# Retention attention and a SwiGLU block on one core: the second tile's attention ticks placed at other steps

## The chip, the cores and the metric

The kernel runs on one core of one Trainium2 chip. The metric is the device time of one execution in microseconds. Engines are named as in the profile: PE (matmuls), DVE (VectorE), ACT (ScalarE), POOL (GpSimd) and SP (the queue that issues most loads and stores).

## The reference

Eight batches of eight heads, 576 positions of 64 values each, go through a retention layer: scores `q k^T / 8`, multiplied with a decay that falls with the distance, times `v`. The result, seen as 4608 tokens of 512 values, is the input x of a SwiGLU block with 1536 hidden values.

```python
ret = scale * (q @ k.transpose(0, 1, 3, 2)) * Dmat      # Dmat[h, i, j] = gamma[h] ** (i - j) for i >= j, else 0
x = (ret @ v).transpose(0, 2, 1, 3).reshape(4608, 512)
g = x @ w_gate
out = (g * sigmoid(g) * (x @ w_val)) @ w_out
```

All data are float32.

## The kernel before

**Attention.** Two heads of a batch make a pair; there are 32 pairs, four to a batch. Each pair is cut into 9 chunks of 64 positions; a running state carries the earlier chunks. The work is pipelined in ticks: `tick(t)` (L675) prepares pair t, does the scores and the new states of pair t-1, and the values of pair t-2. PE's part is emitted at once where the tick stands, in this order: values of pair t-2 from its own scores (L531), new states of t-1 from its k and v (L542), values from earlier states of t-2 (L554, L558), scores of t-1 from qT and kT (L566, L572). It is some 2.2 us of 64x64 matmuls.

The rest of a tick is a list of pieces for the other engines, handed out little by little. For the ticks in question they are, in this order:

- P0: ACT copies the even states (L583), DVE masks the scores (L579, L588), ACT copies the finished values to x (L646, L621);
- P1, in three parts: DVE pairs states up (L593); DVE runs the odd states (three of L598); DVE the even states (L603) and ACT scales k (L506) and, below pair 20, q (L486);
- P2: DVE transposes q into qT (L489);
- P3: DVE transposes k into kT (L489), and SP gets the loads of pair t+2. The one kT buffer serves all pairs.

A tick that begins flushes what is left of the one before.

**SwiGLU.** The tokens are worked through in five tiles; tile 0 is handled apart. In the others the matmuls of a tile are done as a fast bilinear scheme: 26 products per quarter of the hidden values in the up direction (`up_step`, L976, 8 matmuls of 128x256, 1.73 us), three quarters, and then 26 products down (`down_step`, L1030, 12 matmuls, 2.59 us). The tables `UP` and `DOWN` give for each product its PSUM bank, the sums and differences of operands ahead of it, and what is read out of the bank behind it. Reads that take a bank's value are DVE additions (L929) or ACT copies (L926), the hidden values are products of DVE (L1016, L1019) behind an ACT activation (L1013). Sums of operands are L795 and L963 on POOL or DVE. SP also fetches stored operands through a ring of eight places, one at each down step.

**Where the two meet.** Tile 1 (the second tile, `n == 1`) is the one that this change is about: its weight sums are computed while it runs. The first 26 up steps are done without ticks. Here the other 52 are called u0 to u51 (u0 to u25 the second quarter, u26 to u51 the third), and the down steps d0 to d25. Among them stand ticks 12 to 21. Tick 12 has no PE work.

The order in which instructions are emitted is the order on each engine. Around an up step it is: sums for x and weights; the 8 matmuls; if a tick came just ahead, its P0 (`after_tick`); the reads; one part of the next piece (`part_on`), unless the table's line of this step or of the next has five or more reads. The line of the eighteenth step of a quarter (counted from 0) has seven, so u17, u18, u43 and u44 hand out nothing beyond a P0. Around a down step it is: sums of hidden values; 12 matmuls; the fetch; P0 if a tick came just ahead; the reads; and then up to three whole pieces (`go_on(3)`), which is all that a tick has left.

So a tick ahead of u17 leaves P0 at u17, the parts of P1 at u19, u20 and u21, P2 at u22, and P3 at the end of u23.

Of the kernel before, what the change touches and what calls it, by code (L numbers as in the profile page):

```python
# [154 lines left out]
def kernel(  # L155
# [101 lines left out]
    def needed(n):  # L257

        last = (min(starts[n] + TW, NT) - 1) // S
        return last * HP + HP - 1 + 3  # L260
# [547 lines left out]
    for line in OUT_SUMS:  # L808
        i, s = line.split("|")
# [220 lines left out]
    def down_step(n, i):  # L1030
        label, opens, slot, hops, ops = down[i]
        for op in hops:
            add(nc.gpsimd if i % 3 == 1 and op[0] != "nad" else nc.vector, op, hid_view)
        w = operand().rearrange("p (q x) -> p q x", q=NQ)
        lhs = hid_view(slot)
        b = bank(label, i == 0)
        for qd in range(NQ):
            for m in range(2):
                nc.tensor.matmul(b[:, m * TB : (m + 1) * TB], lhs[:, qd, ts(m, P)], w[:, qd],  # L1039
                                 start=(opens and qd == 0 and m == 0), stop=(qd == NQ - 1), skip_group_check=True)  # L1040
        fetch()

        def result(o, src, negative, vector):
            if negative:
                nc.scalar.mul(out=src, in_=src, mul=-1.0)
            d, t = divmod(o, 4)
            rows = starts[n] + t * TB
            nc.sync.dma_start(out=out[rows : rows + TB, d * TB : (d + 1) * TB].rearrange("(m p) d -> p m d", p=P),
                              in_=src.rearrange("p (m d) -> p m d", m=2))

        if n + 1 == NTILE and i + 1 == N:
            _, o, a = ops.pop()
            d, t = divmod(int(o), 4)
            at, rows = part[int(a)], starts[n] + t * TB
            assert ops == [["add", a, "b", a]]
            for m, queue in enumerate((nc.sync, nc.scalar)):
                nc.vector.tensor_tensor(out=at[:, ts(m, TB)], in0=b[:, ts(m, TB)], in1=at[:, ts(m, TB)], op=ALU.add)
                queue.dma_start(out=out[rows + m * P : rows + (m + 1) * P, d * TB : (d + 1) * TB], in_=at[:, ts(m, TB)])
            return
        after_tick()  # L1060
        reads(ops, b, False, result)
        at = 2 * (i - (N - 1 - X_FIRST // 2))
        if 0 <= at < X_FIRST and n + 1 < NTILE:
            x_sums(n + 1, at, at + 2, True)
        go_on(3)


    def merge(*lists):
        merged = [((i + d) / len(l), j, f) for j, (d, l) in enumerate(lists) for i, f in enumerate(l)]
        for _, _, f in sorted(merged, key=lambda e: e[:2]):  # L1070
            f()
# [73 lines left out]
    done = FIRST  # L1145

    def spread_tick(t):
        tick(t, FIRST, NP, True, lambda: next_load(t))
        fresh.append(t)

    ticks = lambda a, b: [lambda t=t: spread_tick(t) for t in range(a, b)]
    for n in range(1, NTILE):
        upto = needed(n + 1) if n + 1 < NTILE else done
        cut = (done + upto + (n == 1) * 2) // 2
        ups = [lambda qd=qd, i=i: up_step(n, qd, i) for qd in range(NQ) for i in range(N)]
        if n == 1:

            for i in range(N):
                ups.pop(0)()
                if i in (6, 14):  # L1160
                    wait = nc.sync.nop()
                    tc.add_manual_dep(wait.ins, stepped[-1].ins.name,
                                      mybir.DependencyInfo(mybir.DependencyClass.Sync, mybir.DependencyReason.DATA), reason="loads in turn")
                    load(FIRST + i // 14)
        downs = [lambda i=i: down_step(n, i) for i in range(N)]
        merge((0.0, ticks(done, cut)), (0.5, ups))
        if n == 1:

            for i, f in reversed(list(zip((2, 7, 13, 19), ticks(cut, upto), strict=True))):
                downs.insert(i, f)  # L1170
            merge((0.5, downs))
        else:
            merge((0.0, ticks(cut, upto)), (0.5, downs))
        done = upto

# [29 lines left out]
```

## Time and profile before

| | us |
|---|---|
| median of 3 runs | 1048.08 |
| lowest and highest | 1047.18, 1050.52 |
| the profiled execution, its own time | 1047.18 |
| its span, first to last instruction | 1045.5 |
| PE busy | 1027.6 (98%) |
| DVE, POOL, ACT busy | 653.9, 401.9, 297.2 |
| granted TensorE clock, mean | 0.998 |

Start times of PE's work in the profiled execution, in us from the span's start: u0 at 222.54, tick 13 at 238.17, tick 14 at 253.38, u24 at 269.03, tick 15 at 272.65, u26 at 275.63, tick 16 at 291.37, tick 17 at 307.64, d0 at 327.22, tick 18 at 332.49, tick 19 at 347.90, tick 20 at 366.40, tick 21 at 384.40, the end of the tile near 405.6.

How to read the lines that follow: a timeline line has the start and the length in us, the engine, the line of the kernel, the operation, what it writes and reads, its shape and how many instructions were merged; in brackets the idle time of the engine ahead of it and what ended that. A line of stretches has, after the stretch and its length, busy time and count of PE, PE's weight loads, DVE, ACT and POOL, then the granted clock, the share of the DMA engines and GB/s.

### The profile page before, as it was taken

To read this page: it belongs to the slowest core of one execution; us is meant where nothing else is said; L and a number is where in the kernel's file an instruction comes from. 1 tells how busy PE (TensorE), PEld (TensorE's weight loads), DVE (VectorE), ACT (ScalarE), POOL (GpSimd) and SP (SyncE) were. 2 spreads that over 40 slices of the span, in tenths; PEclk is the share of its full clock that TensorE was granted. 3 is DMA by queue.
4 is the path that set the end of the run, shared out by engine and by line. 5 is a ranking of instruction groups with operands and counts; after the bars stand their busy time and mean duration, and the time that the engine had idled before them with its cause. 6 is when DMAs were issued, how large, how long until landed. Compare 5 with 4: busy or idle time off the path is not lost.

```text
span 1045.5 us, 21496 instructions
## 1 busy us (share of the span) xinstructions
PE 1027.6 (98%) x8448; PEld 843.9 (81%) x8448; DVE 653.9 (63%) x1063; ACT 297.2 (28%) x646; POOL 401.9 (38%) x347
## 2 busy tenths in 40 slices
PE   7999999999999999999999999999999999999998
PEld 6444555888888888888888888888888888888887
DVE  4678878777769757555357786535476644344644
ACT  3466423243533222232322102223120022231110
POOL 2002367767476035612223048312250483222505
PEclk9999999999999999999999999999999999999999
DMA  9999867776678887665676777545554565555653
GB/s 248 242 283 258 198 197 267 207 212 182 186 204 227 239 249 200 193 178 149 176 220 159 214 182 220 154 136 155 154 174 140 153 200 152 152 153 161 181 161 101
DMA packets 310380, 199.10 MB, mean 190 GB/s; under 512 B 220168, under 2 KB 254984, under 8 KB 310280
## 3 DMA queue, kind: packets, MB, share of 16 engines
q1 hardware_dynamic: 279000, 161.51, 57.2%
q10 hardware_dynamic: 31280, 36.22, 10.4%
q8 instruction: 67, 1.10, 0.5%
q14 instruction: 33, 0.27, 0.1%
HBM read 157.56 MB, written 40.11 MB: 189 GB/s over the span
## 4 chain that ended last, share of the span: by engine, by line
PE 76%; DVE 4%; DMA 1%; ACT 0%; issue 0%; POOL 0%; ACTq 0%; DVEq 0%
PE bankC L992 12%; PE bankE L992 12%; PE bankA L992 11%; PE bankB L992 11%; PE bankA L1039 6%; PE bankB L1039 6%; PE bankC L1039 6%; PE bankE L1039 6%; DVE rest L929 1%; PE outer L531 1%; PE inner L572 1%; DVE state L598 1%; PE outer L558 1%; PE inner L542 1%; DVE arena L1016 1%
## 5 line engine op out<-in xcount | busy, mean ns | idle before, releaser
L929 POOL TENSOR_TENSOR rest<-rest 128x512 f32<-128x512 f32 x65 | 92.1, 1421 | 296.7 <-DVE rest L929 277.9
L1013 ACT ACTIVATE io<-rest 128x256 f32<-128x256 f32 x180 | 74.9, 416 | 305.3 <-DVE rest L929 259.1
L992 PE MATMUL bankA<-rest,arena 128*128 128x256 f32 x544 | 128.9, 380 | 1.8 <-DVE rest L929 1.0
L992 PE MATMUL bankC<-rest,arena 128*128 128x256 f32 x544 | 129.2, 380 | 1.4 <-DVE rest L929 1.4
L795 POOL TENSOR_TENSOR arena<-arena 128x512 f32<-128x512 f32 (+1 forms) x72 | 112.5, 1574 | 38.3 <-DMA up<-arena 22.4
L992 PE MATMUL bankE<-rest,arena 128*128 128x256 f32 x512 | 121.4, 380 | 1.0 <-DVE rest L929 1.0
L992 PE MATMUL bankB<-rest,arena 128*128 128x256 f32 x512 | 121.2, 379 | 0.0
L992 PEld LDWEIGHTS bankA<-rest,arena 128*128 128x128 f32 x544 | 103.0, 190 | 16.9 <-issue 1.9
L1020 POOL TENSOR_TENSOR arena<-rest,io 128x256 f32<-128x256 f32 x72 | 52.1, 729 | 167.3 <-ACT io L1013 167.3
L992 PEld LDWEIGHTS bankC<-rest,arena 128*128 128x128 f32 x544 | 102.8, 190 | 16.3 <-issue 1.8
L992 PEld LDWEIGHTS bankE<-rest,arena 128*128 128x128 f32 x512 | 97.0, 190 | 14.7 <-DVE rest L929 1.4
L992 PEld LDWEIGHTS bankB<-rest,arena 128*128 128x128 f32 x512 | 97.0, 190 | 13.4 <-issue 0.2
L795 POOL TENSOR_TENSOR rest<-rest 128x256 f32<-128x256 f32 (+1 forms) x66 | 67.8, 1048 | 100.9 <-DVE rest L419 61.2
L929 DVE TENSOR_TENSOR rest<-bankB,rest 128x512 f32<-128x512 f32 x72 | 48.8, 686 | 65.6 <-PE bankB L992 49.7
L929 DVE TENSOR_TENSOR rest<-bankC,rest 128x512 f32<-128x512 f32 x72 | 48.9, 687 | 64.6 <-PE bankC L992 45.9
L929 DVE TENSOR_TENSOR rest<-bankA,rest 128x512 f32<-128x512 f32 x72 | 48.8, 685 | 61.1 <-PE bankA L992 43.5
L929 DVE TENSOR_TENSOR rest<-bankE,rest 128x512 f32<-128x512 f32 x71 | 48.2, 687 | 60.5 <-PE bankE L992 46.1
L1016 DVE SCALAR_TENSOR_TENSOR arena<-rest,io 128x256 f32<-128x256 f32 x84 | 57.8, 689 | 11.1 <-ACT io L1013 10.9
L1039 PE MATMUL bankC<-arena 128*128 128x256 f32 x252 | 58.4, 381 | 0.3 <-issue 0.3
L1039 PE MATMUL bankB<-arena 128*128 128x256 f32 x252 | 58.3, 381 | 0.0
L1039 PE MATMUL bankA<-arena 128*128 128x256 f32 x252 | 58.0, 380 | 0.2 <-DVE arena L795 0.2
L1039 PE MATMUL bankE<-arena 128*128 128x256 f32 x252 | 57.9, 379 | 0.0
(189 smaller groups left out, 1632.4 us busy)
## 6 DMA issues: line engine op xcount, KB each, us to landing
arena<-up SPq DMA_DIRECT2D x234, 256.0 KB, 2.7
arena<-dn SPq DMA_DIRECT2D x104, 384.0 KB, 3.9
up<-arena ACTq DMA_DIRECT2D x78, 256.0 KB, 4.1
dn<-rest SPq DMA_DIRECT2D x78, 128.0 KB, 1.9
out_dram<-rest SPq DMA_DIRECT2D x31, 256.0 KB, 3.7
qk<-in_q_dram SPq DMA_DIRECT2D x108, 72.0 KB, 2.4
qk<-in_k_dram SPq DMA_DIRECT2D x108, 72.0 KB, 3.1
rest<-in_moe_w_out_dram ACTq DMA_DIRECT2D x6, 1024.0 KB, 5.4
```

Source lines behind the costliest of these rows:

```text
L531: m = nc.tensor.matmul(value(i, hl, c), s["v"][rows, at], ret[rows, c % 2 if whole(i) else hl, c // 2], start=start, stop=start, skip_grou ...
L542: nc.tensor.matmul(z[half[hl], r, c], s["kn"][chunk(i, hl, 2 * c + r, i < HP)], s["v"][rows, at], start=True, stop=True, skip_group_check= ...
L558: nc.tensor.matmul(xr[half[hl]] if c + 1 == NC else value(i, hl, c), state[half[hl], c, :], s["qT"][half[hl], column(i, hl, c)], start=Fal ...
L572: nc.tensor.matmul(sc[chunk(i, hl, 2 * c + r)[0], r if whole(i) else hl, c], kT[half[hl], at], qT[half[hl], at], start=True, stop=True, sk ...
L598: nc.vector.scalar_tensor_tensor(out=at[:, c], in0=at[:, c - 1], scalar=step[:, HP + p : HP + p + 1], in1=at[:, c], op0=ALU.mult, op1=ALU.add)
L795: eng.tensor_tensor(out=dst, in0=srcs[0], in1=srcs[1], op=ALU.add if op[0] == "add" else ALU.subtract)
L929: eng.tensor_tensor(out=at(op[1]), in0=at(op[2]), in1=at(op[3]), op=ALU.add if op[0] == "add" else ALU.subtract)
L992: m = nc.tensor.matmul(b[:, gv * TB : (gv + 1) * TB], w[:, gv, ts(c, P)], rhs[:, c, :], start=(opens and gv == 0 and c == 0), stop=(c == 1 ...
L1013: nc.scalar.activation(out=s, in_=src[:, 0:TB], func=AF.Silu, scale=-1.0 if negative else 1.0)
L1016: return lambda: nc.vector.scalar_tensor_tensor(out=dst, in0=src[:, TB : 2 * TB], scalar=-1.0, in1=s, op0=ALU.mult, op1=ALU.mult)
L1020: nc.gpsimd.tensor_tensor(out=dst, in0=src[:, TB : 2 * TB], in1=s, op=ALU.mult)
L1039: nc.tensor.matmul(b[:, m * TB : (m + 1) * TB], lhs[:, qd, ts(m, P)], w[:, qd], start=(opens and qd == 0 and m == 0), stop=(qd == NQ - 1), ...
```

## The change

In tile 1 the ticks are no longer merged evenly into the up steps, but put ahead of steps given by a list; the list for the down steps gets other numbers. Other tiles are merged as they were. No instruction is added or taken away, and a tick's pieces keep their order.

```diff
-        merge((0.0, ticks(done, cut)), (0.5, ups))
         if n == 1:
 
-            for i, f in reversed(list(zip((2, 7, 13, 19), ticks(cut, upto), strict=True))):
+            for i, f in reversed(list(zip((0, 10, 17, 24, 34, 44), ticks(done, cut), strict=True))):
+                ups.insert(i, f)
+            merge((0.5, ups))
+            for i, f in reversed(list(zip((4, 8, 14, 18), ticks(cut, upto), strict=True))):
                 downs.insert(i, f)
             merge((0.5, downs))
         else:
+            merge((0.0, ticks(done, cut)), (0.5, ups))
             merge((0.0, ticks(cut, upto)), (0.5, downs))
```

The step that each tick stands ahead of:

| tick | 12 | 13 | 14 | 15 | 16 | 17 | 18 | 19 | 20 | 21 |
|---|---|---|---|---|---|---|---|---|---|---|
| before | u0 | u9 | u17 | u26 | u35 | u43 | d2 | d7 | d13 | d19 |
| after | u0 | u10 | u17 | u24 | u34 | u44 | d4 | d8 | d14 | d18 |

## The prediction

> **What bounds the kernel now.** I read the page first: TensorE (PE) is busy 98% of the span, and it carries 76% of the chain that ended last. So only a change in PE's waits can move the time. The page:
>
> ```profile
> PE 1027.6 (98%) x8448; PEld 843.9 (81%) x8448; DVE 653.9 (63%) x1063; ACT 297.2 (28%) x646; POOL 401.9 (38%) x347
> ```
>
> Then the view of waits, PE alone (line, releaser, total us, times, longest):
>
> ```profile
> PE bankC L992 <- DVE rest L929: 1.4, 1, 1.4
> PE bankA L992 <- DVE rest L929: 1.0, 1, 1.0
> ...
> PE outer L566 <- DVE kT L489: 0.5, 1, 0.5
> ...
> PE bankA L1039 <- DVE arena L795: 0.2, 1, 0.2
> ```
>
> The timeline places these four inside the stretch that the change rearranges (238 to 407 us): 1.04 ahead of u24, 0.51 inside tick 15, 1.44 ahead of u50, 0.24 ahead of d11. Another 0.34 us stands inside d20. Everything the change could give back is therefore 1.04 + 0.51 + 1.44 + 0.24 + 0.34 = 3.57 us. About 0.3% (3.14 us) is what a measurement of this kernel can tell from no change, so a visible gain would need nearly all of it.
>
> Last I read the timelines around tick 15, PE first (start, duration):
>
> ```profile
> 266.10 1.89 PE L992 MATMUL bankB<-x_odd,arena 128*128 128x256 f32 x8
> 269.03 1.97 PE L992 MATMUL bankA<-rest,arena 128*128 128x256 f32 x8 [1.04 <-DVE rest L929]
> 270.83 1.89 PE L992 MATMUL bankC<-x_odd,arena 128*128 128x256 f32 x8
> 272.65 0.46 PE L531 MATMUL outer<-ret,v 64*64 64x64 f32 x16
> ...
> 274.91 0.27 PE L566 MATMUL outer<-qT,kT 64*64 64x64 f32 x2 [0.51 <-DVE kT L489]
> ...
> 275.63 1.99 PE L992 MATMUL bankE<-rest,arena 128*128 128x256 f32 x8
> ```
>
> These are u23, u24, u25, the start of tick 15, its scores, and u26. The scores come as soon as VectorE (DVE) has transposed k of pair 14 into kT, and that is already 0.51 us too late. DVE's own queue there:
>
> ```profile
> 264.93 2.75 DVE L598 SCALAR_TENSOR_TENSOR state<-state,tab 128x64 f32<-128x64 f32 x3
> 267.61 1.27 DVE L929 TENSOR_TENSOR rest<-bankA,rest 128x512 f32<-128x512 f32 x2
> ...
> 271.13 0.78 DVE L489 STREAM_TRANSPOSE qT<-qk 128x576 f32<-128x576 f32 x1 [0.59 <-ACT qk L486]
> ...
> 272.73 1.43 DVE L1019 TENSOR_TENSOR arena<-rest,io 128x256 f32<-128x256 f32 x1
> 274.09 0.77 DVE L489 STREAM_TRANSPOSE kT<-qk 128x576 f32<-128x576 f32 x1
> ```
>
> and the ACT line that scales pair 14's k:
>
> ```profile
> 269.30 0.95 ACT L506 ACTIVATE kn<-kn,tab 128x256 f32<-128x256 f32 x2
> ```
>
> All of this is tick 14's late pieces and the reads of u20 to u23. None of it waits for anything that PE does after u23. So the kT transpose ends at 274.09 + 0.77 = 274.86 wherever tick 15 stands.
>
> **Tick 15, two steps earlier (ahead of u24 instead of u26).** Tick 14 stays at u17, and its last piece (kT) is given out at the end of u23: it is now the instruction right ahead of tick 15. PE ends u23 at 266.10 + 1.73 = 267.83 and enters tick 15 at once. After 0.3 us its new states need the scaled k, which ACT has at 269.30 + 0.95 = 270.25: some 2.0 us idle. About 1.5 us of small matmuls later it stands at the scores and waits from about 271.75 to 274.9: 3.15 us. The two waits make 5.15 us where 1.04 + 0.51 = 1.55 stood. Behind the blocked scores stand all later matmuls. By start times: the scores still begin at 274.91 and a step follows at 275.63, but that step is u24 and no longer u26. The two steps once done during the wait now come after it: 1.83 (275.63 to 277.46) + 1.73 = 3.56, less 0.10 since u26 no longer follows a tick: **+3.46 us**. DVE, ACT and SP lose nothing: they are not the bound for the next 10 steps (DVE is idle 3.97 us at 280), and the loads that tick 15 issues on SP go out two steps earlier, with only loads for later ticks behind them.
>
> **The clock.** PE would be nearly empty from 268.2 to 274.9, 1.5 us of work in 6.7. In the trace of before the granted clock fell once, after a gap of 1.65 us at 21.76 among small matmuls:
>
> ```profile
> 20.00:24.00 4.00, 2.35 (x55) 1.90 (x51) 2.50 (x8) 1.50 (x4) 1.95 (x3) 0.97 1.17 298
> 24.00:28.00 4.00, 3.62 (x129) 3.40 (x121) 2.41 (x6) 3.31 (x7) 0.36 (x1) 0.60 1.05 281
> ```
>
> The clock is the third number from the end: 0.97, then 0.60. That lost (0.03 + 0.40) x 4 = 1.72 us of full-clock time. Gaps of 1.03, 1.04 and 1.44 us amid dense matmuls lost none. The new gap is longer than all of them, so I take one such drop, **+1.7 us**; bounds 0 (no drop) and 3.4 (twice as long). The Trainium skill, "TensorE: Matmul & The Clock Gate", section "Why this matters for your kernels", speaks against this change: it asks for no PE idle gap above about 3 us, since one idle window puts the clock to half. By that rule a drop is near certain; by the row of 1.44 alone it would be open.
>
> **Ticks 13, 16 and 17 (u9 to u10, u35 to u34, u43 to u44).** Tick 13's chain runs beside a POOL burst (its L598 took 3.93 us), but DVE's reads there are not waited for by PE before u16, six steps on: 0. Tick 16's inputs are done by u28 or u29, five steps ahead: 0. Tick 17 moves past a step, but u43 and u44 give out none of the later pieces in either version (the line of eighteen has seven reads), so only its masks and copies move, into time that DVE idles there (1.62 and 0.59 us). Its L598 still stands just ahead of the double read of u47, so the 1.44 us ahead of u50 stays: 0, bounds -1.44 and +0.4.
>
> **Ticks 18 to 21 (d2 to d4, d7 to d8, d13 to d14, d19 to d18).** In the down steps all pieces of a tick leave at once. Tick 19's used to delay d8's four sums, which cost 0.24 us ahead of d11; now those sums are ahead of it and that wait goes. What is late next: d9's sum, which d12 reads. DVE by rows: the sums end near 356.4; masks to L603 take 2.6; from L588 the ACT work up to L486 takes 4.07 (351.62 to 355.69 before), so the transposes end near 362.7; d9's sum, 0.96, near 363.7, where d12 would start at 363.2: a wait of 0.5. Net **+0.3 us**, bounds -0.24 and +1.2. SP: the loads of pairs 20 and 21 now go out with kT near 346 and 363 and hold the queue 9.1 and 8.1 us as before; the fetch behind the second serves d17 at 379, and would be issued near 371, plus 3.9 to land: hidden with 4 us left.
>
> **Sum.** 3.46 + 1.72 + 0.3 = 5.5 us. The profiled execution took 1047.18 us (span 1045.5 and 1.7 around it), so it becomes 1052.7; it was the fastest of three, and on their median of 1048.08 the sum is 1053.6.
>
> **Rivals.**
> - *Wait without a clock drop.* 3.46 + 0.3 = 3.8: 1051.8. For it: the three dense gaps without loss. Against it: 5.15 us idle in 6.7.
> - *DVE's chain gets shorter.* L598 took 2.75 us beside POOL's sums (busy 262.28 to 267.60) and 0.93 with POOL idle (278.85). Tick 13's move lets POOL's burst start earlier; if POOL were out of the way by 265, kT would end 1.8 us sooner: 3.46 - 1.8 + 0.3 = 2.0, or 1050.0. Against it: at 260.89 POOL waits for a read of DVE's that has not moved. The Trainium skill, "SBUF — State Buffer", section "Who interferes with whom", says that a DVE instruction with two SBUF inputs and a GpSimd one that reads SBUF block each other for a whole instruction; with POOL's order unchanged that keeps the 2.75.
> - *Not slower: the early tick removes the wait at u24 and meets no new one.* -1.55: 1046.5. This is decided by one time: kT would have to end by 274.86 - 3.46 = 271.4, before qT's transpose (271.13, waiting for ACT) is even done. All waits gone would be 1048.08 - 3.57 = 1044.5.
>
> **Chances.** Wait with a drop 0.58, without 0.22, shorter chain 0.12, no wait 0.05, all waits gone 0.03. Slower by over 0.3% (above 1051.2): nearly all of the first, three quarters of the second, little of the third: 0.76. Faster (below 1044.9): 0.04, the last and some noise. Within: 0.20. The range runs from the shorter chain, 1050.0, to the first case with a doubled drop and the upper bound at d12: 1053.6 + 1.7 + 0.9 = 1056.2, say 1056.5. It leaves out the last two and some of the ends.
>
> **What would show it.** In the profile after: a PE wait of L566 on kT L489 near 3 us, and one of L542 on ACT kn L506 near 2 us, both between 267 and 276; no wait ahead of u24; a granted clock below 1 in the 4 us that follow; the 1.4 us ahead of u50 still there. I am wrong if kT's transpose ends before 272, if the wait is there and the span grows by under 2 us, or if the largest new wait lies in the down steps.

## The result, and the profile after

| | before | after |
|---|---|---|
| median of 20 runs | 1048.05 us | 1053.08 us |
| lowest, highest | 1045.26, 1051.72 | 1049.77, 1054.97 |
| span of the profiled execution | 1045.5 us | 1050.0 us |

The ratio of the times is 1.0041, 95% interval 1.003 to 1.0052: the changed kernel is slower by some 4 to 5 us. The prediction was 1053.6 us. Two executions, one of the kernel before (1800.92 us) and one of run 10 (1195.66 us), had mean granted clocks of 0.56 and 0.85 and are left out of the ratios below.

The page of the changed kernel, the line of busy times and that of the granted clock over the 40 slices. PE is at 98% as before; in the clock there is one dent, the eleventh slice, from 262 to 289 us:

```profile
PE 1029.2 (98%) x8448; PEld 845.8 (81%) x8448; DVE 654.3 (62%) x1063; ACT 297.6 (28%) x646; POOL 402.8 (38%) x347
...
PEclk9999999999899999999999999999999999999999
```

The view of waits, PE alone, from 222 to 327 us, the changed kernel (before, this answer was 1.4 and 1.0 for L929 and 0.5 for kT):

```profile
PE outer L566 <- DVE kT L489: 3.1, 1, 3.1
PE inner L542 <- ACT kn L506: 1.4, 1, 1.4
```

The wait of 1.44 us for L929 lies just behind that window now, at 329.92. The two new ones are both in tick 15. PE's timeline there, the changed kernel:

```profile
266.94 1.89 PE L992 MATMUL bankB<-x_odd,arena 128*128 128x256 f32 x8
...
270.66 1.08 PE L542 MATMUL inner<-v,kn 64*64 64x64 f32 x29 [1.43 <-ACT kn L506]
...
275.71 0.37 PE L566 MATMUL outer<-qT,kT 64*64 64x64 f32 x2 [3.11 <-DVE kT L489]
...
276.98 3.42 PE L992 MATMUL bankA<-rest,arena 128*128 128x256 f32 x8
280.23 1.89 PE L992 MATMUL bankC<-x_odd,arena 128*128 128x256 f32 x8
281.96 1.89 PE L992 MATMUL bankE<-rest,arena 128*128 128x256 f32 x8
```

Read it from above: u23, tick 15, u24, u25, u26. The scores (L566) wait 3.11 us for kT; u24 takes 3.25 us to the start of u25, where a first step behind a tick took 1.83 before. DVE's kT transpose, the reason of the wait, is where it was (before 274.09; this execution is 0.84 late at u0):

```profile
274.89 0.77 DVE L489 STREAM_TRANSPOSE kT<-qk 128x576 f32<-128x576 f32 x1
```

The clock in the stretches of 4 us (the third number from the end), the changed kernel; before, all of these stretches have 1.00:

```profile
268.00:272.00 4.00, 2.44 (x80) 1.78 (x82) 3.42 (x8) 2.63 (x7) 0.42 (x1) 1.00 0.18 66
272.00:276.00 4.00, 0.89 (x48) 0.75 (x42) 3.66 (x5) 1.12 (x3) 2.57 (x2) 0.63 0.41 134
276.00:280.00 4.00, 4.00 (x43) 3.33 (x39) 0.82 (x2) 1.59 (x5) 0.09 (x1) 0.51 0.69 111
280.00:284.00 4.00, 4.00 (x20) 3.52 (x19) 2.85 (x8) 0.95 (x3) 0.00 (x0) 1.00 0.39 107
```

Where the time went, by start times of PE's steps in the two profiles:

| stretch | before | after | difference |
|---|---|---|---|
| u0 to u23 | 43.56 | 43.56 | 0 |
| u23 to u26 | 9.53 | 15.02 | +5.49 |
| u26 to d0 | 51.59 | 51.49 | -0.10 |
| d0 to the third tile's first step | 80.63 | 79.97 | -0.66 |
| u0 to the third tile's first step | 185.31 | 190.04 | +4.73 |

The rest of the 4.5 us between the spans lies outside: u0 began 0.84 later, and 1.07 came back after the tile (a wait of 0.75 at 510 is in the profile of before alone).

### The profile page after: what moved, and what is told of

It is laid out like the page before. It is cut to its first block, busy times and chain, and to the rows that moved or that the text cites. A ratio compares the mean times of both kernels' runs of the same rounds, so it can differ in the third digit from the quotient of the medians.

```text
span 1050.0 us, 21500 instructions
## 1 busy us (share of the span) xinstructions
PE 1029.2 (98%) x8448; PEld 845.8 (81%) x8448; DVE 654.3 (62%) x1063; ACT 297.6 (28%) x646; POOL 402.8 (38%) x347
## 4 chain that ended last, share of the span: by engine, by line
PE 77%; DVE 3%; DMA 1%; POOL 1%; issue 0%; ACT 0%; ACTq 0%; DVEq 0%; POOLq 0%
PE bankC L992 12%; PE bankE L992 12%; PE bankA L992 12%; PE bankB L992 11%; PE bankB L1039 7%; PE bankC L1039 6%; PE bankE L1039 6%; PE bankA L1039 6%; PE outer L531 1%; DVE rest L929 1%; PE inner L572 1%; DVE state L598 1%; PE outer L558 1%; PE inner L542 1%; DMA up<-arena 1%; DVE arena L1016 1%
## 5 line engine op out<-in xcount | busy, mean ns | idle before, releaser
L929 POOL TENSOR_TENSOR rest<-rest 128x512 f32<-128x512 f32 x65 | 92.0, 1420 | 294.9 <-DVE rest L929 276.0
L795 POOL TENSOR_TENSOR arena<-arena 128x512 f32<-128x512 f32 (+1 forms) x72 | 113.1, 1583 | 46.1 <-DMA up<-arena 31.4
L795 POOL TENSOR_TENSOR rest<-rest 128x256 f32<-128x256 f32 (+1 forms) x66 | 67.5, 1044 | 102.4 <-DVE rest L419 62.4
L929 DVE TENSOR_TENSOR rest<-bankC,rest 128x512 f32<-128x512 f32 x72 | 48.9, 686 | 64.4 <-PE bankC L992 45.3
L929 DVE TENSOR_TENSOR rest<-bankB,rest 128x512 f32<-128x512 f32 x72 | 48.8, 686 | 63.1 <-PE bankB L992 48.8
L929 DVE TENSOR_TENSOR rest<-bankA,rest 128x512 f32<-128x512 f32 x72 | 48.9, 687 | 62.3 <-PE bankA L992 45.0
L929 DVE TENSOR_TENSOR rest<-bankE,rest 128x512 f32<-128x512 f32 x71 | 48.2, 687 | 63.3 <-PE bankE L992 49.3
```

The source lines that it names most:

```text
L795: eng.tensor_tensor(out=dst, in0=srcs[0], in1=srcs[1], op=ALU.add if op[0] == "add" else ALU.subtract)
L929: eng.tensor_tensor(out=at(op[1]), in0=at(op[2]), in1=at(op[3]), op=ALU.add if op[0] == "add" else ALU.subtract)
```

## The experiments

All kernels differ from the changed one in a few characters or, in runs 6 and 7, in four added lines; the diffs below show what was altered, and "..." stands for the rest of a line. "Stretch" is the time from u0 to the third tile's first step in the kernel's profile (185.31 before, 190.04 changed). It is shown beside the timed ratio because the part ahead of it, which no kernel here alters, ends anywhere between 221.2 and 228.6 us.

**1. The changed kernel again**, on the chip of runs 2, 3 and 6.

> The changed kernel as it is, so that the other kernels of this group stand beside it on the same chip. Both theories: about 5.0 us over the kernel before, with PE waits of some 1.4 us for the scaled k and 3.1 us for kT in tick 15.

Ratio 1.003 (1.0009 to 1.0051), median 1052.26 against 1049.49. Stretch 417.50 - 227.27 = 190.23. The waits in tick 15 are 1.3 and 3.1 us, u24 takes 3.57 us. As expected in the profile; the timed runs give 3 us (interval 0.9 to 5.4) where 5 was expected.

**2. Tick 15 alone moved**

```diff
-zip((0, 9, 17, 26, 35, 43), ...    and (2, 7, 13, 19)
+zip((0, 9, 17, 24, 35, 43), ...    and (2, 7, 13, 19)
```

> The kernel before, with tick 15 alone moved from u26 to u24; all other ticks stand as before. Theory 'tick 15': the whole loss is here, 3.46 us of order and some 1.95 of clock: 5.4 us over the kernel before, a little more than the changed kernel. Rival 'many moves': the loss is spread over the moved ticks, so this one gives less than 3 us.

Ratio 1.0039 (1.0018 to 1.0061), stretch 412.31 - 221.85 = 190.46, which is 5.15 over before: the whole loss from one tick. The view of waits has the same two lines:

```profile
PE outer L566 <- DVE kT L489: 3.1, 1, 3.1
...
PE inner L542 <- ACT kn L506: 1.6, 2, 1.4
```

**3. Tick 15 alone put back**

```diff
-zip((0, 10, 17, 24, 34, 44), ...    and (4, 8, 14, 18)
+zip((0, 10, 17, 26, 34, 44), ...    and (4, 8, 14, 18)
```

> The changed kernel, with tick 15 alone put back to u26. Theory 'tick 15': what is left of the change gives -0.4 us (the waits of 0.24 ahead of d11 and of some 0.5 inside d20 go, one of 0.37 ahead of d12 comes), so 1047.6, not to be told from the kernel before. Rival 'many moves': at least 1.5 us slower than the kernel before.

Ratio 0.9987 (0.9966 to 1.0008): not to be told from before. Stretch 410.75 - 226.23 = 184.52, or -0.79. The other seven moves together cost nothing. "Many moves" is out.

**4. Tick 15 one step later than changed**

```diff
-zip((0, 10, 17, 24, 34, 44), ...
+zip((0, 10, 17, 25, 34, 44), ...
```

> The changed kernel, with tick 15 at u25, one step later than changed and one earlier than before. Theory: one step (1.73 us) is behind the wait instead of two, so kT is waited for some 2.3 us and the scaled k not at all; the wait ahead of u24 (1.04) is back. Without a clock drop 1.73 - 0.4 = 1.3 us over the kernel before, with one 3.2; no drop is likelier, since the idle time comes in two parts with 1.7 us of dense matmuls between them. Rival: the loss is all or nothing, 0 or 5 us.

Stretch 415.28 - 227.45 = 187.83, or +2.52. The timed ratio of 1.0001 (0.998 to 1.0023) does not tell between 0 and 2.4 us. In the profile the wait for kT is 2.23, as worked out, but the clock did drop, which I had held the less likely:

```profile
279.63 0.27 PE L566 MATMUL outer<-qT,kT 64*64 64x64 f32 x2 [2.23 <-DVE kT L489]
...
280.45 3.54 PE L992 MATMUL bankC<-x_odd,arena 128*128 128x256 f32 x8
283.83 1.89 PE L992 MATMUL bankE<-rest,arena 128*128 128x256 f32 x8
```

u25 takes 3.38 us instead of 1.83. So the parts are 1.73 (one step behind the wait) + 1.55 (clock), less 0.7 in the down steps: 2.6. In the profiles the order loss goes by steps, as the theory says. The drop is shown for this one execution only: at 1053.63 us it was the slowest of the twelve, with a mean clock of 0.995 where the others have 0.996 to 1.0, and the timed interval (-2.1 to 2.4 us) has no room for the 3.2 us that was worked out with a drop.

**5. kT earlier, tick 15 still ahead of u24**

```diff
-zip((0, 10, 17, 24, 34, 44), ...
+zip((0, 9, 15, 24, 34, 44), ...
```

> The changed kernel, with tick 15 still at u24, but tick 13 at u9 and tick 14 at u15 instead of u17, so that tick 14's pieces are given out two steps earlier and kT at u21 instead of u23. Theory 'kT': tick 15 ahead of u24 costs nothing by itself; with kT and the scaled k done in time both its waits go, no clock drop follows, and the three waits of L598's delay at u24 (1.04) and of kT (0.51) go as well: about -1.9 us with the down steps' -0.4, so 1046.1. Rival 'place': the place ahead of u24 is bad whatever kT does, so 3 us or more over the kernel before.

Ratio 1.0002 (0.9982 to 1.0022); stretch 408.33 - 223.53 = 184.80, or -0.51. Tick 15 stands where the change puts it, and the loss is gone: no wait for kT or for the scaled k, and a granted clock of 1.00 from 264 to 284. PE's scores:

```profile
272.63 0.22 PE L566 MATMUL outer<-qT,kT 64*64 64x64 f32 x2
```

kT is done at 271.62, 1.0 us ahead of them. This settles "kT" against "place". The gain of 1.9 us was not there, though, since POOL's sums became late for u22. DVE's and POOL's timelines of this kernel:

```profile
258.00 3.24 DVE L598 SCALAR_TENSOR_TENSOR state<-state,tab 128x64 f32<-128x64 f32 x3
261.16 0.68 DVE L929 TENSOR_TENSOR rest<-bankA,rest 128x512 f32<-128x512 f32 x1
...
262.59 1.27 DVE L929 TENSOR_TENSOR rest<-bankC,rest 128x512 f32<-128x512 f32 x2
...
270.87 0.75 DVE L489 STREAM_TRANSPOSE kT<-qk 128x576 f32<-128x576 f32 x1
```

```profile
263.94 1.42 POOL L929 TENSOR_TENSOR rest<-rest 128x512 f32<-128x512 f32 x1 [1.56 <-DVE rest L929]
265.32 4.28 POOL L795 TENSOR_TENSOR arena<-arena 128x512 f32<-128x512 f32 x3
```

L598 was slow beside POOL again (3.24 us), now ahead of the reads of u17 and u18; POOL's L929 waits for the second of them, so its three weight sums run from 265.32 to 269.60 (262.28 to 266.38 before, where u0 was 0.99 earlier). u22 waits 1.30 us for the first of them and starts at 266.82; u23 waits 0.31 more for a read of DVE's.

**6. PE kept busy during the wait**

```diff
+        if t == 15:
+            for _ in range(13):
+                nc.tensor.matmul(inner[:, 0, 0:256], ident, near.rearrange("p h i -> p (h i)")[:, 0:256],
+                                 start=True, stop=True, skip_group_check=True)
         if lo <= t - 1 < hi:
             scores(t - 1, t - 2 < lo)
```

> The changed kernel, with 13 useless matmuls of 128x256 ahead of tick 15's scores (they write the place in PSUM that the scores then fill). At 0.216 us each they take 2.8 us, about the 3.1 us for which PE waits there. Theory 'clock': 1.95 of the 5.4 us lost at u26 are a clock drop that this idle time sets off; with PE kept busy the clock stays up, so the kernel gets faster by about 1.9 us than the changed one, to some 3.1 us over the kernel before, although work is added. Rival 'order only': the 2 us behind the wait are something else, so the time is that of the changed kernel or up to 1 us more.

Ratio 1.0042 (1.0018 to 1.0066), stretch 419.13 - 228.60 = 190.53. My size was wrong: each call makes two instructions, so the filler took 5.8 us and ran past kT. It still tells something: the clock stayed at 1.00 in every stretch from 268 to 292 (the one that holds u24 is shown), and u24 took 1.83 us:

```profile
275.72 1.08 PE L542 MATMUL inner<-v,kn 64*64 64x64 f32 x29 [1.28 <-ACT kn L506]
...
277.59 5.88 PE L707 MATMUL inner<-near,ident 128*128 128x256 f32 x26
...
283.40 0.27 PE L566 MATMUL outer<-qT,kT 64*64 64x64 f32 x2
...
284.13 1.99 PE L996 MATMUL bankA<-rest,arena 128*128 128x256 f32 x8
285.96 1.89 PE L996 MATMUL bankC<-x_odd,arena 128*128 128x256 f32 x8
```

```profile
284.00:288.00 4.00, 4.00 (x32) 3.49 (x23) 2.01 (x5) 2.01 (x6) 0.00 (x0) 1.00 0.57 99
```

From u23 (272.16) to tick 15's scores (283.40) it needs 11.24 us, the changed kernel 8.77: 2.47 us more. From u23 to u26 (287.69) it needs 15.53 against 15.02: only 0.51 more. The 1.96 us between are the clock. The timed runs agree: the mean granted clock of the twelve is 0.998, in the twelve of run 1 on the same chip 0.995.

**7. The same with 6 calls**

```diff
-            for _ in range(13):
+            for _ in range(6):
```

> The changed kernel with 6 useless matmuls of 128x256 ahead of tick 15's scores. Each call makes two instructions of 0.216 us, which the run with 13 calls showed, so these take 2.6 us and end before kT does. Theory 'clock': tick 15's scores start when kT is done as in the changed kernel, the clock stays up, and from u0 to the second tile's end the profile is 1.95 us shorter than the changed kernel's 190.04 us, so 188.1; in time some 3 us over the kernel before. Rival 'order only': 190 us again.

The profile is inconclusive. Ratio 1.003 (1.0015 to 1.0044), stretch 417.23 - 227.49 = 189.74, near the rival's number. But in it the clock dropped already behind the first wait, which was longer than in the others (1.95 us for the scaled k, up to 275.31; the clock is 1.00 up to 275.5 and 0.75 in the next half microsecond), so the filler itself ran slow (12 instructions in 3.2 us), and no profile shows a filler of the right length at full clock:

```profile
272.00:276.00 4.00, 1.92 (x31) 1.27 (x33) 4.00 (x7) 1.98 (x5) 1.06 (x1) 0.97 0.13 51
276.00:280.00 4.00, 4.00 (x88) 3.69 (x85) 3.42 (x6) 1.76 (x5) 1.93 (x2) 0.60 0.45 148
```

The timed runs lean to the theory. The profiled execution was the slowest of the twelve and had the lowest mean clock (0.995; the twelve together 0.998), and the medians, 1050.50 against 1048.01, are 2.5 us apart (interval 1.6 to 4.6), where the theory had some 3 and the rival the 4.7 us of the changed kernel's stretch.

**8. Ticks 14 and 17 two steps earlier**

```diff
-zip((0, 10, 17, 24, 34, 44), ...
+zip((0, 9, 15, 26, 35, 41), ...
```

> A version meant to beat both: ticks 14 and 17 at u15 and u41 (the fifteenth step of a quarter, counted from 0, instead of the seventeenth), tick 13 at u9, tick 15 at u26, tick 16 at u35, the down steps' ticks as changed. DVE's odd states (L598) then run at the sixteenth step, well ahead of the double read of the twenty-first, and kT comes two steps sooner. Theory: the waits of 1.04 ahead of u24, 1.44 ahead of u50 and 0.51 in tick 15 go, 0.4 more in the down steps: 3.4 us under the kernel before, 1044.7. Rival: DVE is as late at another read, and at least one wait of over 0.5 us stands at another of these steps; then within 1.5 us of the kernel before.

Ratio 1.0031 (1.0011 to 1.0051), stretch 412.68 - 225.24 = 187.44, or +2.13. The rival was right in kind but not in size: it allowed 1.5 us, and the timed interval is 1.2 to 5.3. All waits that this version was to remove are gone, and others came: twice 1.30 us for POOL's sums (L795, the releaser that run 5 shows too), and 1.55 us ahead of d3 for an operand of the ring. SP's timeline shows that one: the loads of tick 17, which wait for kT, now stand ahead of fetches that d3 needs.

```profile
319.87 5.75 SPq L890 DMA_DIRECT2D arena<-dn  x3
328.00 2.44 SPq L293 DMA_DIRECT2D qk<-in_q_dram  x4
...
336.08 7.50 SPq L890 DMA_DIRECT2D arena<-dn  x9
```

**9. All ticks away from the full steps**

```diff
-zip((0, 10, 17, 24, 34, 44), ...
+zip((0, 4, 12, 26, 32, 38), ...
```

> Ticks 12 to 17 at u0, u4, u12, u26, u32 and u38, so that no piece of a tick stands in the steps eighteen to twenty-five of a quarter, where DVE is at its fullest; the down steps' ticks as changed. Theory: with DVE's chain free there, the waits ahead of u24 (1.04) and u50 (1.44) and in tick 15 (0.51) go, and no fetch of the ring stands behind a load at u47: 3.4 us under the kernel before, 181.9 us from u0 to the second tile's end (185.31 before). Rival: POOL's or the fetches' waits come in their place, as in the run with ticks 14 and 17 at the fifteenth step; then 185 or more.

Ratio 1.0075 (1.005 to 1.0101), stretch 413.89 - 221.23 = 192.66. A miss: d0 waits 6.31 us for its operand. The loads of tick 17 are emitted earlier, but SP gets them off only from 315.4 to 326.2, and the first fetch of the down steps goes out at 326.35. The clock fell behind this wait too (0.55 from 332 to 336): d0 takes 4.40 us to the start of d1 instead of 2.59.

**10. The odd states after the double read**

```diff
-zip((0, 10, 17, 24, 34, 44), ...
+zip((0, 9, 20, 28, 36, 46), ...
```

> Ticks 12 to 17 at u0, u9, u20, u28, u36 and u46: the odd states (L598) come after the double read of the twenty-first step instead of ahead of it, when POOL's sums are done. Theory: the waits of 1.04 and 1.44 go, kT of pair 14 is given out at u24, four steps ahead of tick 15: 3.0 us under the kernel before, some 182.3 us from u0 to the second tile's end. Rival: DVE is late at the quarter's last reads instead, and a wait of 1 us or more comes at the next quarter's first steps or at d0 to d5.

Ratio 0.9972 (0.9955 to 0.9988), median 1045.64 against 1048.01: faster than the kernel before (the changed one, slower than that, was not timed beside it). Stretch 407.29 - 224.91 = 182.38, where 182.3 was expected. From u0 to d0 PE waits for nothing that the view of waits shows. L598 comes behind the double read and takes 1.37 us, and kT is done 3.3 us ahead of tick 15's scores at 278.78:

```profile
266.95 1.29 DVE L929 TENSOR_TENSOR rest<-bankA,rest 128x512 f32<-128x512 f32 x2 [0.33 <-PE bankA L992]
268.15 1.37 DVE L598 SCALAR_TENSOR_TENSOR state<-state,tab 128x64 f32<-128x64 f32 x3
...
274.72 0.76 DVE L489 STREAM_TRANSPOSE kT<-qk 128x576 f32<-128x576 f32 x1
```

The price is a wait of 0.87 us for an ACT copy ahead of d3.

## Why the prediction was right, point by point

- **Tick 15, +3.46.** Right in cause and size. The scores started with the end of kT (275.71 after 274.89 + 0.77 = 275.66), and u24 and u25 came behind them. Of +5.49 from u23 to u26, 1.97 are the clock, which leaves 3.52. The two idle times were 1.43 and 3.11 where the prediction had 2.0 and 3.15; the first was too large by 0.6, which changes nothing, since the second absorbs it. Runs 2, 3 and 5 show that this tick is the loss and kT the reason.
- **The clock, +1.7.** Right that it falls; it cost 1.97. It is read off the two items behind the wait: from the scores to u24 1.27 instead of 0.72, and u24 3.25 instead of 1.83. Run 6 shows that it goes when PE has work. That the size came so near is in part luck. Counted as the prediction counted the earlier drop, the two rows of the changed kernel lose (0.37 + 0.49) x 4 = 3.44 us, its upper bound; but 1.48 of these stand in the row up to 276, where PE waited for kT until 275.71, and cost next to nothing. Nor can the 3.11 us of that wait have decided. In stretches of half a microsecond the clock is 1.00 up to 273.0, 0.57 in the next and 0.50 after that, while PE's small matmuls end at 272.61: it fell 0.9 us into the wait at the latest, less than the 1.44 us that passed without a drop ahead of u50. So the wait of 1.43 us and the small matmuls behind it probably counted too, though not alone, since in run 6 the clock stayed up behind a wait of 1.28; how much each counts is not shown. The Trainium skill's rule ("TensorE: Matmul & The Clock Gate", section "Why this matters for your kernels") pointed the right way; its limit of about 3 us is not a safe bound in this case, since in profiles of run 4 and run 7 the clock fell behind gaps of 2.23 us (with one of 0.86 us some 3.6 us ahead of it) and 1.95 us.
- **Ticks 13, 16 and 17, 0.** Right: 43.56 and 43.56 ahead of u23, 51.59 and 51.49 from u26 to d0, and the 1.44 ahead of u50 stayed. One word on the text above: the table's line of the eighteenth step has six reads, not seven; five are enough for what was said.
- **Down steps, +0.3.** The one term with the wrong sign: -0.66. The wait that was to come did come: d9's sum ended at 368.80 + 0.92 = 369.72, and d12 started at 369.81, 0.37 later than its predecessor allowed (0.5 foretold; the view of waits has 0.21 of it and names no releaser). The 0.24 ahead of d11 went. By start times the one at d12 cost 0.45 with the step behind it, and the one ahead of d11 had cost 0.51, which the prediction took for its idle time of 0.24 alone. What the sum had left out is the stop inside d20, which the prediction names among what the change could give back: 3.20 us from d20 to d21 before, 2.59 after. Together that is -0.51 + 0.45 - 0.61 = -0.67. The stop stands in the two profiles with tick 21 ahead of d19 (before, and run 2 with 3.02) and is not in that of the changed kernel. What it is the profile does not say; it names only issue.
- **The rivals.** "DVE's chain gets shorter": no, L598 beside POOL took 2.75 us again. "Not slower" was decided by the time that it named: kT would have had to end 3.46 us sooner, and in run 5, where it ended 4.2 us sooner (48.09 us after u0 instead of 52.32), the loss was gone.

The sum was 5.5; the profiles gave 4.73 within the tile, the medians 5.0.

## What to carry to other kernels

An instruction placed right behind its producer in program order gets its input as late as the producer's whole queue is; before moving work ahead, find the end of the last input on its own engine and count what then stands behind the wait. A full engine stalled for a few us can pay twice, once for the wait and once for the clock after it, though of the clock only what falls on work counts. The place that helped was not the earliest one but the one that put the slow instructions (L598 beside POOL) behind the reads that others wait for, and with every step moved its loads on the shared queue have to be followed too: two of four placements failed by that or by POOL's chain.

## What the runs showed that I had not expected

- An idle time of 2.23 us was followed by a granted clock of 0.57 over 4 us (the profile of run 4); ahead of it stood one step of dense matmuls, the small matmuls of the tick and, before these, a gap of 0.86 us. Gaps of 1.44 us (before, ahead of u50) and 1.55 us (run 8, ahead of d3) were not followed by a drop.
- The part of the program that no kernel here touches varies more than the change moves: the first up step of tile 1 started between 174.49 and 181.50 us in the twelve profiles. Differences of 2 us needed the profile's own stretch beside the timed runs.
